# The second filter stage of batches 1 to 7: plain fp32 on four 64x64 squares of TensorE in place of 96x96 fp32r hi/lo products

## The chip, the cores and the metric

One core of a Trainium2 chip runs the whole program in one launch. The metric is device time in microseconds (us), from timed runs of one execution each; beside them stands one profiled execution, from which every duration here comes.

## The reference, cut to what matters

`x` is 8 batches of 3072 x 256 in fp32. Each of its columns is filtered along the sequence in the frequency domain, and two dense blocks of a feed-forward kind follow, token by token:

```
X = np.fft.rfft(x, axis=1)
Y = X * (filt_r + 1j * filt_i)[None, :, :]
y = np.fft.irfft(Y, n=3072, axis=1)
# block 1, on 24576 tokens
h = y @ w_in                        # 256 -> 1024
solu = h * softmax(h);  ln = (solu - mean) / sqrt(var + 1e-06) * g_ln
x2 = ln @ w_out                     # 1024 -> 256
# block 2
h = x2 @ w_in2                      # 256 -> 2048
out = (h / (1 + exp(-1.702 * h))) @ w_out2
```

## The kernel before, in words

**The transform.** 3072 is 128 x 24, and the real transform is done in two steps of small matrices. The first step multiplies 128 points by a 128 x 128 matrix (`step1`, line 493 in plain fp32, line 451 in three fp32r products); its result goes to a DRAM tensor `a_d`. That leaves 64 *slots* of 48 values (24 real, 24 imaginary) for the second step, whose matrices differ from slot to slot. Two slots make a *group* of R = 96 rows, 32 groups in all. Of a 96 x 96 matrix of a group half the entries are zero, since the two slots do not mix.

For each group of a pair of batches (1 and 2, 3 and 4, 5 and 6, then 7 alone) the second step does this: load the two matrices and the filter (`gt`) and the data (`bt`); split matrices and data in a high fp32r part and the rest (`split_m`, `split_a`: ScalarE copies, GpSimd subtracts); `forward`, one product of three fp32r matmuls at line 451 (high by high, rest by high, high by rest), into a PSUM tile of the tag `m`; two VectorE operations that weigh it with the filter (`xs`, `pr`); `swap`, two DMAs that exchange the halves of `xs`; `weigh`, an addition; `split_y`; `inverse`, again a product of three matmuls; a ScalarE copy `z` out of PSUM; `store_z`, a DMA to `z_d`. Both batches of a pair lie side by side, so a matmul has 512 columns (256 for batch 7). Batch 0 has its own class, `EarlyFilter`, in the opening.

**What follows.** A *piece* is 256 tokens; there are 96. `First` (one object for each piece) takes `z_d` through the last small transform (`y`, line 742) and block 1: `hidden` (line 760), softmax and norm on ScalarE and VectorE, a transpose by way of DRAM (`shuffle`, `gather`, `turn`), `project` (line 842), `x2_add`. `Second` does block 2 for two pieces at a time: `hidden` (line 913), `tanh`, `gate`, `split_hi`, `split_lo`, `output` (line 954).

**The order.** Nothing is scheduled at run time. Every step is put in a list with a planned time (`at`), the list is sorted once, and each engine gets its instructions in that order; an engine waits at its next instruction until the data is there. A unit of that time is a sixteenth of a piece. The tables FILTER and DENSE hold the planned times of the filter's steps: the second stage of batches 1 and 2 (DENSE) is spread over 8 pieces, four groups to a piece, and that of the later batches (FILTER) over 16 pieces, two groups to a piece. The tag `m` has two PSUM buffers, shared by the filter's products, by `y` and by `project`.

Nearly all loads and stores are issued by SyncE (SP), one after the other; a DMA whose data is not ready holds up those behind it.

Of the kernel before, what the change touches and what calls it, by code (L numbers as in the profile page):

```python
# [10 lines left out]
F32 = mybir.dt.float32  # L11
F32R = mybir.dt.float32r
# [14 lines left out]
NG = NSLOT // 2  # L27
FF1, FF2 = 1024, 2048
# [3 lines left out]
Q = 32  # L32
# [40 lines left out]
    "slots": (-0.4, 3.33, 4.15, 16.59),  # L73
    "first": (-9.95, -6.06, -1.85, 0.69),
    "second": (-7.28, -3.52, -2.25, 0.52, 1.17, 4.88, 12.1, 15.71, 20.24),
# [4 lines left out]
    "start": 15.68,  # L80
    "slots": (0.57, 4.18, 8.25, 12.02),
    "second": (-5.2, -2.91, -2.91, -0.1, 2.39, 5.33, 7.45, 10.13, 14.61),
# [51 lines left out]
def dft_constants():  # L134
# [15 lines left out]
    fwd1, inv1 = fwd1.reshape(N1, N1), inv1.reshape(N1, N1)  # L150
# [37 lines left out]
    fwd2 = fwd2.reshape(NG, R, R)  # L188
    inv2 = inv2.reshape(NG, R, R)
# [7 lines left out]
    def spread(m):  # L197
# [11 lines left out]
        [fwd1, inv1, turned, np.eye(N1), -np.eye(N1), blocks.reshape(P, -1)], 1)  # L209
    return [np.ascontiguousarray(a, np.float32) for a in (dft1, mats, sgn)]  # L210
# [3 lines left out]
def fft_filter_solu_gelu(  # L214
# [46 lines left out]
    mats_in = dft1[:, 4 * N1 + R:]  # L261
# [4 lines left out]
    sgn_sb = cst.tile([R, 2], F32, name="sgn_sb")  # L266
# [186 lines left out]
    filtered = [0] * B  # L453

    class Filter:
        pools = {"gt": [(p3, "gt")], "bt": [(p3, "bt")], "az": [(p2, "az")]}
        send = nc.sync.dma_start

        def __init__(self, batches):
# [10 lines left out]
            self.stored = 0  # L470
# [34 lines left out]
        def load2(self, g):  # L505
            self.load_gt(g)
            self.load_bt(g)

        def load_bt(self, g):
            assert self.stored == self.steps  # L510
            bt = self.tile("bt", g, [R, self.nb, D], F32)
            dma(out=bt, in_=self.a_d[:, g].rearrange("b r d -> r b d"))
            self.t[g]["bt"] = bt

        def load_gt(self, g):
            gt = self.tile("gt", g, [R, 2 * R + 2 * D], F32)
            dma(out=gt, in_=groups[:, g])
            fl = gt[:, 2 * R:].rearrange("p (t n) -> p t n", t=2)
            both = [R, self.nb, D]
            self.t[g] = dict(  # L520
                m=gt[:, :2 * R], fl=fl,
                fr=fl[:, 0:1].to_broadcast(both), fi=fl[:, 1:2].to_broadcast(both))

        def split_m(self, g):
            v = self.t[g]
# [3 lines left out]
            v["fwd"], v["inv"] = ([mt[:, i, j * R:(j + 1) * R] for i in range(2)] for j in range(2))  # L529

        def split_a(self, g):
            self.t[g]["a"] = split(self.t[g]["bt"], nc.gpsimd)

        def forward(self, g):
            v = self.t[g]
            f = ps_m.tile([R, self.nb, D], F32, tag="m", name="f2")
            product(f, v["fwd"], v["a"])
            xs = p2.tile([R, self.nb, D], F32, tag="xs", name="xs")
            pw = p2.tile([R, 2, self.nb, D], F32, tag="pw", name="pw")
            pr, v["xw"] = pw[:, 0], pw[:, 1]  # L540
            nc.vector.scalar_tensor_tensor(
                out=xs, in0=f, scalar=sgn_sb[:, min(g, 1):min(g, 1) + 1], in1=v["fi"],
                op0=ALU.mult, op1=ALU.mult)
            nc.vector.tensor_tensor(pr, f, v["fr"], op=ALU.mult)
            v.update(xs=xs, pr=pr)

        def swap(self, g):
            v = self.t[g]
            dma(out=v["xw"][:2 * N2], in_=v["xs"][2 * N2:])
            dma(out=v["xw"][2 * N2:], in_=v["xs"][:2 * N2])  # L550

        def weigh(self, g):
            v = self.t[g]
            nc.vector.tensor_tensor(v["pr"], v["xw"], v["pr"], op=ALU.add)

        def split_y(self, g):
            self.t[g]["y"] = split(self.t[g]["pr"], nc.vector)

        def inverse(self, g):
            v = self.t[g]  # L560
            f = ps_m.tile([R, self.nb, D], F32, tag="m", name="f3")
            product(f, v["inv"], v["y"])
            z = p2.tile([R, self.nb, D], F32, tag="az", name="z")
            nc.scalar.copy(out=z, in_=f)
            v["z"] = z

        def store_z(self, g):
            self.send(out=self.z_d[:, g].rearrange("b r d -> r b d"), in_=self.t.pop(g)["z"])
            for b in self.batches:
                filtered[b] += 1  # L570

    class EarlyFilter(Filter):
# [4 lines left out]
        def __init__(self, batches):  # L577
# [11 lines left out]
            bts = [pool.tile([P, 2 * D], F32, tag=tag, name="bt")  # L589
# [22 lines left out]
        def load_gt(self, g):  # L612
# [5 lines left out]
            if g % 2 == 0:  # L618
                dma(out=fl[:R // 2], in_=groups[:R // 2, g:g + 2, 2 * R:])
            if g == 0:  # L620
                dma(out=fl[H:W, 0], in_=groups[R // 2:, g, 2 * R:])
# [56 lines left out]
        def store_z(self, g):  # L678
# [4 lines left out]
            filtered[0] += 1  # L683

    def plan_filter(batches, first, second, early=None):


        f = Filter(batches) if batches[0] else EarlyFilter(batches)
        for i in range(f.steps):
# [415 lines left out]
```

## Time and profile before

| | |
|---|---|
| timed runs, three | 3632.44, 3633.64, 3636.73 us |
| median | 3633.64 us |
| the profiled execution: span from first to last instruction | 3631.5 us |
| its own time outside the span | not recorded; the median of the timed runs lies 2.1 us above the span |
| granted TensorE clock, mean | 0.994 |

The profile gives for each engine the time in which it had an instruction in work. A TensorE matmul's record begins when it is handed to the array and ends when its last column has left it, so records overlap: the distance from start to start is what a matmul costs, not the length of its record. An fp32r product is one matmul instruction, a plain fp32 product is two.

### The profile page before, as it was taken

What the parts mean: (1) busy time and instruction counts of PE and PEld (TensorE: products, weight loads), DVE (VectorE), ACT (ScalarE), POOL (GpSimd) and SP (SyncE); (2) the same over time, 40 slices, a digit from 0 to 9 for tenths busy, and PEclk for the clock granted to TensorE, in tenths of its full rate; (3) what the DMA queues carried; (4) which work ended last, traced back from release to release, by engine and by line L of the source; (5) the groups of instructions that cost most, each with busy time, mean ns of one, the idle gap of its engine ahead of it and who ended that gap; (6) DMA issues with size and microseconds to landing.
All of it is one profiled execution on the core that took longest, in us unless ns stands there. A gap on an engine that the chain in (4) does not pass through costs nothing.

```text
span 3631.5 us, 50437 instructions
## 1 busy us (share of the span) xinstructions
PE 3569.6 (98%) x16828; PEld 2942.3 (81%) x16828; DVE 2677.4 (74%) x3964; ACT 2034.3 (56%) x3672; POOL 795.5 (22%) x1315
## 2 busy tenths in 40 slices
PE   6899999999999999999999999999999999999999
PEld 4478888888888888888888888888888888888887
DVE  6878876677777777667777777667777776676665
ACT  3656655555555555555555555555555555555553
POOL 3033322212222221222222222211212111111110
PEclk8999999999999999999999999999999999999999
DMA  9855543434343433443434343333333332222221
GB/s 261 262 159 147 162 131 125 134 110 121 114 125 116 123 113 113 128 128 105 125 114 125 112 122 109 123 106 112 107 101 105 108 108 80 78 79 78 77 82 27
DMA packets 384597, 431.47 MB, mean 119 GB/s; under 512 B 143520, under 2 KB 294304, under 8 KB 384336
## 3 DMA queue, kind: packets, MB, share of 16 engines
q1 hardware_dynamic: 378704, 421.82, 39.3%
q10 hardware_dynamic: 5632, 6.42, 0.6%
q8 instruction: 132, 2.16, 0.3%
q14 instruction: 129, 1.06, 0.1%
HBM read 229.89 MB, written 176.16 MB: 112 GB/s over the span
## 4 chain that ended last, share of the span: by engine, by line
PE 92%; DVE 3%; DMA 2%; issue 1%; ACT 1%; SPq 0%; POOL 0%; DVEq 0%; ACTq 0%; POOLq 0%
PE o L954 28%; PE h L913 28%; PE x L842 15%; PE h L760 13%; PE f L451 5%; PE yt L742 2%; DMA a_d<-az 1%; PE f L671 0%; DMA e<-e_d 0%; DVE x2s L863 0%; PE f L493 0%; PE f L652 0%; DVE ob L965 0%; DVE e L785 0%; DVE gl L937 0%
## 5 line engine op out<-in xcount | busy, mean ns | idle before, releaser
L913 PE MATMUL h<-x2s,w 128*128 128x512 f32 (+1 forms) x4704 | 1179.4, 386 | 1.9 <-DVE th L925 1.3
L913 PEld LDWEIGHTS h<-x2s,w 128*128 128x128 f32 x4704 | 864.1, 188 | 180.6 <-DVE x2s L863 4.0
L954 PE MATMUL o<-gh,w 128*128 128x512 f32 (+1 forms) x3136 | 961.7, 388 | 4.2 <-DVE ob L965 3.3
L931 ACT CAST gh<-th 128x512 fp32r<-128x512 f32 x768 | 476.2, 620 | 684.2 <-DVE th L925 677.0
L954 PEld LDWEIGHTS o<-gh,w 128*128 128x128 f32 x3136 | 577.1, 188 | 121.2 <-issue 7.8
L954 PE MATMUL o<-gl,w 128*128 128x512 f32 (+1 forms) x1568 | 606.6, 387 | 2.0 <-DVE gl L937 2.0
L937 DVE TENSOR_TENSOR gl<-th,gh 128x512 fp32r<-128x512 f32 x768 | 559.3, 728 | 32.2 <-ACT gh L931 32.1
L925 DVE SCALAR_TENSOR_TENSOR th<-th,h 128x512 f32<-128x512 f32 x768 | 521.0, 678 | 29.1 <-ACT th L920 28.7
L920 ACT ACTIVATE th<-h 128x512 f32<-128x512 f32 x768 | 456.3, 594 | 107.4 <-PE h L913 106.7
L854 DVE TENSOR_TENSOR x_sum<-x,x_sum 128x256 f32<-128x256 f32 x192 | 81.5, 425 | 584.2 <-ACT x_sum L853 584.2
L842 PE MATMUL x<-u,w_hi 128*128 128x512 f32 x1536 | 383.1, 392 | 0.3 <-DVE u L833 0.3
L954 PEld LDWEIGHTS o<-gl,w 128*128 128x128 f32 x1568 | 294.8, 188 | 65.4 <-DVE gl L937 6.0
L842 PEld LDWEIGHTS x<-u,w_hi 128*128 128x128 f32 x1536 | 289.8, 189 | 62.6 <-DVE u L833 1.0
L776 POOL TENSOR_SCALAR q<-se 128x1 f32<-128x1 f32 x192 | 43.9, 229 | 1207.6 <-ACT e L772 1202.1
L805 DVE TENSOR_SCALAR e<-e,nmu,rs 128x1024 f32<-128x1024 f32 x192 | 160.7, 837 | 161.2 <-POOL rs L800 159.4
L853 ACT COPY x_sum<-x 128x256 f32<-128x256 f32 x192 | 71.0, 370 | 370.7 <-PE x L842 369.8
L796 ACT ACTIVATE h<-e,nmu 128x1024 f32<-128x1024 f32 x192 | 215.0, 1120 | 91.1 <-POOL nmu L788 91.0
L446 POOL TENSOR_TENSOR fl<-bt,fh 96x512 fp32r<-96x512 f32 (+1 forms) x128 | 175.2, 1368 | 365.1 <-ACT fh L445 346.5
L822 DVE STREAM_TRANSPOSE ut<-e 128x1024 f32<-128x1024 f32 x192 | 237.4, 1237 | 10.0 <-DMA e<-e_d 9.8
L766 DVE TENSOR_REDUCE nmx<-h 128x1 f32<-128x1024 f32 x192 | 234.3, 1221 | 13.6 <-PE h L760 13.5
L760 PE MATMUL h<-w_hi,xh 128*128 128x512 f32 x768 | 242.0, 396 | 0.0
L772 ACT ACTIVATE e<-h,nmx 128x1024 f32<-128x1024 f32 x192 | 214.2, 1116 | 44.6 <-DVE nmx L766 44.1
(99 smaller groups left out, 4691.1 us busy)
## 6 DMA issues: line engine op xcount, KB each, us to landing
e_d<-e SPq DMA_DIRECT2D x192, 512.0 KB, 3.0
e<-e_d SPq DMA_DIRECT2D x768, 128.0 KB, 3.0
gt<-in_groups SPq DMA_DIRECT2D x128, 264.0 KB, 3.7
zr<-z_d SPq DMA_DIRECT2D x96, 256.0 KB, 2.7
out<-ob SPq DMA_DIRECT2D x764, 32.0 KB, 1.6
bt<-a_d SPq DMA_DIRECT2D x112, 192.0 KB, 4.0
xin<-in_x SPq DMA_DIRECT2D x84, 256.0 KB, 3.4
a_d<-az SPq DMA_DIRECT2D x84, 256.0 KB, 2.7
```

Source lines behind the costliest of these rows:

```text
L760: nc.tensor.matmul(hs, xx[:, c, a * P:(a + 1) * P], ww[:, c, f * 512:(f + 1) * 512], start=(m == 0 and c == 0), stop=(m == 2 and c == 1))
L766: nc.vector.tensor_reduce(out=nmx, in_=self.h[a], op=ALU.max, axis=AX.X, negate=True)
L772: nc.scalar.activation(out=e, in_=self.h[a], func=AF.Exp, bias=self.v[a], accum_out=se)
L796: nc.scalar.activation(out=self.h.pop(a), in_=e, func=AF.Square, bias=nmu, accum_out=ssq)
L822: nc.vector.transpose(out=self.ut[a].rearrange("p k (i t) -> p k i t", t=Q), in_=self.e.pop(a).rearrange("p (i k f) -> p k i f", i=P // Q, ...
L842: nc.tensor.matmul(self.x2[c][:, :n].rearrange("p i t -> p (i t)"), w2[f][:, kk, c * P:(c + 1) * P], self.u[:, kk, :n].rearrange("p i a t ...
L913: nc.tensor.matmul(self.part(t, j), ww[:, c, f * P:(f + 1) * P], xx[..., c, :], start=(m == 0 and c == 0), stop=(m == 2 and c == 1))
L920: nc.scalar.activation(out=th, in_=self.t[d], func=AF.Tanh, scale=1.702)
L925: nc.vector.scalar_tensor_tensor(out=self.g[d], in0=self.g[d], scalar=1.0, in1=self.t.pop(d), op0=ALU.add, op1=ALU.mult)
L931: nc.scalar.copy(out=gh, in_=self.g[d])
L937: nc.vector.tensor_tensor(gl, th, gh, op=ALU.subtract)
L954: nc.tensor.matmul(o, ww[:, h, f], self.part(gg, j), start=(f == 0 and m == 0), stop=(f == K2 - 1 and m == 2))
```

## The change

For batches 1 to 7 the second stage goes by *quads* of four slots (two groups), q = 0 to 15:

- The four 48 x 48 matrices of a quad are stored so that each stands in its own 64 x 64 square of the array: slot w of group h uses rows from 64h and columns from 64w. `squares` issues four plain fp32 matmuls, one for each square, with 64 output columns, 48 rows (forward) or 64 (inverse) and 512 moving columns. The two that share their rows' half write to one PSUM tile, so a call takes both buffers of the tag `m`.
- Between forward and inverse, real and imaginary parts lie at distances of 32 partitions. `cross` (twice for a quad) is the pair of VectorE operations of before, on 128 partitions; `swap` is four DMAs of 32 partitions for each `cross`; `weigh` is unchanged in kind.
- `split_m`, `split_a` and `split_y` are gone.
- A quad is loaded by one DMA for the matrices, four for the filter (into one tile `fl_sb`, which is not doubled) and two for each batch for the data, and stored by four DMAs.
- The tables FILTER and DENSE give new planned times; DENSE has two quads to a piece, FILTER one. First-stage slots move a little.
- The tile that held the second output block of `finish` and some buffers of `EarlyFilter` change their tags.

```diff
 FILTER = {
-    "slots": (-0.4, 3.33, 4.15, 16.59),
-    "second": (-7.28, -3.52, -2.25, 0.52, 1.17, 4.88, 12.1, 15.71, 20.24),
+    "slots": (-0.05, 3.33, 4.15, 15.38),
+    "second": {"load2": -4.87, "forward": 3.89, "cross": (4.31, 5.2), "swap": (5.0, 5.69), "weigh": (8.13, 9.15), "inverse": 13.25, "copy_z": (14.01, 14.37), "store_z": 15.5},
 }
...
-        pools = {"gt": [(p3, "gt")], "bt": [(p3, "bt")], "az": [(p2, "az")]}
+        pools = {"gt": [(p4, "mt")], "bt": [(p2, "bt")], "az": [(p2, "az")]}
...
-        def split_m(self, g):
-            mt = p4.tile([R, 2, 2 * R], F32R, tag="mt", name="mt")
-            nc.scalar.copy(out=mt[:, 0], in_=v["m"])
-            nc.gpsimd.tensor_tensor(mt[:, 1], v["m"], mt[:, 0], op=ALU.subtract)
...
-        def split_a(self, g):
-            self.t[g]["a"] = split(self.t[g]["bt"], nc.gpsimd)
...
-            f = ps_m.tile([R, self.nb, D], F32, tag="m", name="f2")
-            product(f, v["fwd"], v["a"])
...
+        def load2(self, q):
+            gt = self.tile("gt", q, [P, 4 * H], F32)
+            dma(out=gt, in_=quads[:, q * 4 * H:(q + 1) * 4 * H])
+            fl = fl_sb
+            for w in range(2):
+                for b in range(2):
+                    to, of = w * H + b * Q, (2 * b + w) * N2
+                    dma(out=fl[to:to + N2], in_=groups[of:of + N2, 2 * q:2 * q + 2].rearrange(
+                        "i h (t d) -> i h t d", t=2))
+            bt = self.tile("bt", q, [P, 2, 2, D], F32)
+            for h in range(2):
+                for b in range(self.nb):
+                    dma(out=bt[h * H:h * H + 2 * N2, :, b],
+                        in_=self.a_d[b, 2 * q + h].rearrange("(w p) d -> p w d", w=2))
...
+        def squares(self, m, x, rows):
+            out = [ps_m.tile([P, self.nb, D], F32, tag="m", name="f2") for _ in range(2)]
+            for r in range(2):
+                part = slice(r * H, r * H + rows)
+                for c in range(2):
+                    nc.tensor.matmul(
+                        out[r][c * H:(c + 1) * H], m[part, c * H:(c + 1) * H], x(r, c)[part],
+                        start=True, stop=True, skip_group_check=True)
+            return out
+
+        def forward(self, q):
+            v["f"] = self.squares(v["fwd"], lambda h, w: v["bt"][:, w, :self.nb], 2 * N2)
...
+        def swap(self, q, h):
+            for k in range(P // Q):
+                to, of = k * Q, (k ^ 1) * Q
+                dma(out=v["xw", h][to:to + Q], in_=v["xs", h][of:of + Q])
...
+        def inverse(self, q):
+            v["f"] = self.squares(v["inv"], lambda w, h: v["pr", h], H)
+
+        def copy_z(self, q, w):
+            v["z", w] = p2.tile([P, self.nb, D], F32, tag="az", name="z")
+            nc.scalar.copy(out=v["z", w], in_=v["f"][w])
```

TensorE in the dense stage before, about one piece into it. `f` on line 451 are the filter's products, `h` and `o` block 2, `yt` the last small transform. Each product stands by itself among the others' matmuls:

```order
465 L451 MATMUL f_2806<-fh,mt 96x512 x2
466 L451 MATMUL f_2806<-fl,mt 96x512
467 L913 MATMUL h_2812<-x2s,w_740 128x512 x6
468 L954 MATMUL o<-gh,w_788 128x512 x2
469 L954 MATMUL o<-gl,w_788 128x512
470 L954 MATMUL o<-gh,w_788 128x512 x2
471 L954 MATMUL o<-gl,w_788 128x512
472 L913 MATMUL h_2856<-x2s,w_740 128x512 x6
473 L451 MATMUL f_2864<-fh,mt 96x512 x2
474 L451 MATMUL f_2864<-fl,mt 96x512
475 L742 MATMUL yt<-first,zr 128x128 x4
```

The same engine and stage now. Line 549 is `squares`: `f<-pw` an inverse, `f<-bt` a forward, a row for each of the call's two PSUM tiles; line 888 is `project`, line 806 block 1's `hidden`. Two stretches of one piece:

```order
399 L549 MATMUL f_2421<-pw,gt 64x512 x2
400 L549 MATMUL f_2422<-pw,gt 64x512 x2
401 L549 MATMUL f_2433<-bt,gt 64x512 x2
402 L549 MATMUL f_2434<-bt,gt 64x512 x2
403 L806 MATMUL h<-w_hi,xh 128x512 x2
...
421 L549 MATMUL f_2564<-pw,gt 64x512 x2
422 L549 MATMUL f_2565<-pw,gt 64x512 x2
423 L888 MATMUL x_2570<-u,w_hi 128x512 x8
```

An inverse, which holds both buffers of the tag `m`, now stands directly before a forward in one place of the piece and directly before `project` in the other, and both of these write to the tag `m`.

SyncE's queue in the dense stage before, half a piece. `pw<-xs` is `swap`, `gt` and `bt` the loads, `z_d` the store, `e_d<-e` and `e<-e_d` are `shuffle` and `gather` of block 1:

```order
229 L549 DMA pw<-xs 48x512
230 L550 DMA pw<-xs 48x512
231 L517 DMA gt<-in_groups 96x704
232 L512 DMA bt<-a_d_138 96x2x256
233 L568 DMA z_d_139<-z 96x2x256 x2
```

The same queue now:

```order
182 L577 DMA pw<-xs 32x512 x8
183 L525 DMA gt<-in_dft 128x256
184 L530 DMA fl_sb<-in_groups 24x1024 x4
185 L535 DMA bt<-a_d_138 48x2x256 x4
186 L858 DMA e_d<-e 128x1024
187 L864 DMA e<-e_d 32x4x256 x4
188 L577 DMA pw<-xs 32x512 x8
189 L596 DMA z_d_139<-z 48x2x256 x4
```

From one `zr` load to the next but one, two pieces of the dense stage, the queue held 78 DMAs and now holds 122; in a stretch with one quad to a piece it held 58 and now holds 80.

## Rows read from the trace of the kernel before

**Rows 1.** The page's part 1: busy time, share, instructions.
```profile
PE 3569.6 (98%) x16828; PEld 2942.3 (81%) x16828; DVE 2677.4 (74%) x3964; ACT 2034.3 (56%) x3672; POOL 795.5 (22%) x1315
```

**Rows 2.** Busy time by stretches: length, then busy time of each engine, clock.
```profile
0.00:120.00 120.00, 82.87 (x274) 51.70 (x275) 80.56 (x141) 57.51 (x117) 32.91 (x44) 0.89 0.93 264
...
360.00:480.00 120.00, 120.00 (x562) 98.00 (x561) 103.10 (x151) 74.64 (x141) 45.14 (x55) 1.00 0.54 154
```

**Rows 3.** The chain that ended last: share of the span by line.
```profile
by line: PE o L954 27.6%; PE h L913 27.6%; PE x L842 14.7%; PE h L760 13.1%; PE f L451 5.4%; PE yt L742 2.2%; issue 1.0%; DMA a_d<-az 0.5%; PE f L671 0.4%; DMA e<-e_d 0.4%; DVE x2s L863 0.4%; PE f L493 0.4%; PE f L652 0.4%; DVE ob L965 0.4%
```

**Rows 4.** Groups of instructions by shape, line 451: count after the shape.
```profile
L451 PE MATMUL f<-fh,mt 96*96 96x512 f32 x384 | 121.7, 398 | 0.8 <-POOL mt L528 0.6 <-DVE x_sum L854 0.2
L451 PE MATMUL f<-fh,fwd 128*128 128x512 f32 x120 | 37.8, 396 | 0.0
L451 PE MATMUL f<-fh,mt 96*96 96x256 f32 x128 | 25.0, 282 | 0.0
```

**Rows 5.** TensorE in order of time, two products of 512 columns: start, length.
```profile
1722.45 0.63 PE L451 MATMUL f<-fh,mt 96*96 96x512 f32 x2
...
1723.15 0.62 PE L451 MATMUL f<-fh,mt 96*96 96x512 f32 x2
...
1723.84 0.62 PE L760 MATMUL h<-w_hi,xh 128*128 128x512 f32 x2
```

**Rows 6.** The same, two products of 256 columns.
```profile
2625.89 0.40 PE L451 MATMUL f<-fh,mt 96*96 96x256 f32 x2
...
2626.59 0.63 PE L760 MATMUL h<-w_hi,xh 128*128 128x512 f32 x2
```

**Rows 7.** The same, a plain fp32 product of 512 columns, then fp32r.
```profile
139.53 0.59 PE L493 MATMUL f<-xin,first 128*128 128x512 f32 x1
139.97 0.59 PE L493 MATMUL f<-xin,first 128*128 128x512 f32 x1
140.00 0.80 PE L760 MATMUL h<-w_hi,xh 128*128 128x512 f32 x1
140.63 0.40 PE L760 MATMUL h<-w_hi,xh 128*128 128x512 f32 x1
```

**Rows 8.** The same, an fp32 product that begins after a wait.
```profile
144.58 1.12 PE L412 MATMUL w_lo<-w_top,unit 128*128 128x512 f32 x2 [1.31 <-ACT w L415]
```

**Rows 9.** The same, four fp32 products of 128 columns, and what follows.
```profile
1716.06 1.05 PE L742 MATMUL yt<-first,zr 128*128 128x128 f32 x8
1716.87 0.70 PE L954 MATMUL o<-gh,w 128*128 128x512 f32 x2
```

**Rows 10.** The same at the start of the dense stage: waits in brackets.
```profile
249.29 0.47 PE L451 MATMUL f<-fh,mt 96*96 96x512 f32 x1 [0.63 <-POOL mt L528]
250.52 0.47 PE L451 MATMUL f<-fl,mt 96*96 96x512 f32 x1 [0.76 <-POOL fl L446]
```

**Rows 11.** Groups by shape: busy time, mean ns of one, idle before.
```profile
L564 ACT COPY z<-f 96x512 f32<-96x512 f32 x96 | 55.8, 581 | 44.9 <-PE f L451 42.0
L446 POOL TENSOR_TENSOR fl<-bt,fh 96x512 fp32r<-96x512 f32 x96 | 151.6, 1579 | 240.0 <-ACT fh L445 221.4 <-PE o L954 18.6
```

**Rows 12.** SyncE in the dense stage, in order of time: start, length.
```profile
371.17 0.51 SPq L549 DMA_DIRECT2D pw<-xs  x1
371.73 0.59 SPq L550 DMA_DIRECT2D pw<-xs  x1
```

**Rows 13.** Waits of SyncE's queue from 260 to 560: us in total, times, longest.
```profile
SPq L736 <- DVE x2s L863: 63.8, 8, 9.4
SPq L812 <- DVE e L805: 34.5, 13, 5.5
...
SPq L818 <- DMA e_d<-e: 19.2, 10, 3.6
```

**Rows 14.** The chain that ended last, in order of time: `project` in two successive pieces.
```profile
340.86 2.79 PE x L842 x16
380.32 2.77 PE x L842 x16
```

More of the change, by code (lines that the diff above doesn't have):

```diff
@@ L27 @@
 NG = NSLOT // 2
+NQ = NG // 2
 FF1, FF2 = 1024, 2048
@@ L503, in store_a @@
             self.stored += 1
[L505 to L522, printed above, removed]
@@ L559, in inverse @@
[L559 to L568, printed above, removed]
+            nc.vector.tensor_tensor(pw[:, 0], f, v["fr"][h], op=ALU.mult)
@@ L683, in store_z, with plan_transform @@
             filtered[0] += 1
-    def plan_filter(batches, first, second, early=None):
-        f = Filter(batches) if batches[0] else EarlyFilter(batches)
+    def plan_transform(f, first):
         for i in range(f.steps):
@@ L692, in plan_filter, with plan_early @@
                 at(t, step, i)
+    def plan_early(batches, first, second, early):
+        f = EarlyFilter(batches)
+        plan_transform(f, first)
         for g in range(NG):
             steps = (
-                f.load_bt if early else f.load2, f.split_m, f.split_a, f.forward, f.swap, f.weigh,
+                f.load_bt, f.split_m, f.split_a, f.forward, f.swap, f.weigh,
                 f.split_y, f.inverse, f.store_z)
@@ L701, in plan_filter @@
                 at(t, step, g)
-            if early:
-                in_order(early(g), second(g)[1])
-                at(early(g), f.load_gt, g)
+            in_order(early(g), second(g)[1])
+            at(early(g), f.load_gt, g)
+    def plan_filter(batches, first, second):
+        f = Filter(batches)
+        plan_transform(f, first)
+        for q in range(NQ):
+            v = second(q)
+            in_order(v["load2"], v["forward"])
+            for k in range(2):
+                in_order(
+                    v["forward"], *(v[name][k] for name in ("cross", "swap", "weigh")),
+                    v["inverse"], v["copy_z"][k], v["store_z"])
+            for name in ("load2", "forward", "inverse", "store_z"):
+                at(v[name], getattr(f, name), q)
+            for name in ("cross", "swap", "weigh", "copy_z"):
+                for k in range(2):
+                    at(v[name][k], getattr(f, name), q, k)
     def segments(start, count):
@@ L1018, in fft_filter_solu_gelu, with later, second @@
     at(v["small"][1], lambda: dma(out=sgn_sb, in_=sgn))
-    def dense(g):
-        p, k = divmod(g, len(DENSE["slots"]))
-        return [16.0 * p + DENSE["start"] + DENSE["slots"][k] + d for d in DENSE["second"]]
+    def later(start, steps):
+        def second(q):
+            move = lambda t: [move(x) for x in t] if isinstance(t, tuple) else start + 16.0 * q + t
+            return {name: move(t) for name, t in steps.items()}
+        return second
     def ahead(i):
@@ L1028, in ahead, with dense @@
         return [t + dt for dt in v["more"]]
+    def dense(q):
+        n, k = divmod(q, len(DENSE["second"]))
+        return later(DENSE["start"] + 16.0 * (n - q), DENSE["second"][k])(q)
     plan_filter(together[1], ahead, dense)
@@ L1034, in piece @@
             return 16.0 * ((batches[0] - 2) * NPAIR - 1 + i // 4) + FILTER["slots"][i % 4]
[L1036 to L1041 removed]
+        start = 16.0 * ((batches[0] - 2) * NPAIR - 1 + len(batches) * N2 // 8)
+        plan_filter(
+            batches, lambda i: [piece(i - 4) + d for d in FILTER["first"]],
+            later(start, FILTER["second"]))
     at(v["unit"], load_unit)
```

110 lines of the change are left out of this document (68 added, 42 removed).

## The prediction

> **What bounds the kernel now.** I read the page's first part, then the stretches, then the chain. TensorE has something in work for 98% of the span; the other engines are far from it, VectorE 74%, ScalarE 56%, GpSimd 22% [rows 1]. Records of matmuls overlap, so a full TensorE could hide short waits; the stretches say where there are any. In the first 120 us it is busy for 82.87, at a granted clock of 0.89; from 360 on it is busy for 120.00 of 120.00 at 1.00 [rows 2]. The reader is to see in the chain that its entries are nearly all TensorE lines, and that line 451, the first and second filter stage together, holds 5.4% of 3631.5 us, 196 us [rows 3]. So the change is worth what it does to TensorE's own time, and what it adds in waits of TensorE.
>
> **What it removes.** A product of three fp32r matmuls costs 0.695 us at 512 columns: two of them go from 1722.45 to 1723.84 [rows 5]. At 256 columns two go from 2625.89 to 2626.59, 0.35 each [rows 6]. The second stage has 384 / 2 = 192 products of the first size and 128 / 2 = 64 of the second; 60 more of the first size belong to the first stage and stay [rows 4]. Removed: 192 x 0.695 + 64 x 0.35 = 155.8 us. The chain's 196 less 60 x 0.695 leaves 154.5; the two agree. The splits that go too (GpSimd 1.58 us each [rows 11], ScalarE, VectorE) stand beside a full TensorE and are worth nothing there, but for one place: at the dense stage's start TensorE waits 0.63 and 0.76 us for GpSimd's splits [rows 10], and these 1.4 us go.
>
> **What it adds on TensorE.** Three batch pairs of 16 quads, twice each, are 96 calls of `squares` with 512 columns; batch 7 has 32 with 256. A call is four plain fp32 products, two matmul instructions each. One such product alone costs 0.87 us: its halves begin at 139.53 and 139.97, and behind the second the next matmul's columns end where its successor begins, at 140.63, so they took their 0.23 from 140.40 on [rows 7]. Fewer columns cost in proportion: eight halves of 128 columns take 0.81 us, 0.10 each [rows 9]; 0.44 for 256.
>
> No row shows two matmuls on different squares at once. The ends are one product's time a call, 0.87 us, if the four run side by side, and four, 3.48 us, if they don't. What bears on it is how a matmul is handed over. In [rows 7] the fp32r matmul at 140.00 was handed to the array 0.03 us after the one before it had begun, 0.40 us before it could stream (its record is 0.80 long, its successor's 0.40). So a matmul can wait at the array and needn't hold the queue. If each square has such a place, the second half of one square's product waits there, the next square's first half goes past it, and the call takes 0.87. I take that as likeliest, and 0.87: 96 x 0.87 + 32 x 0.44 = 97.6 us.
>
> The Trainium skill, TensorEngine Tiling (Array Packing), Key Properties, says that tiles operate independently and can load weights and multiply in parallel; by that rule a call is one product's 0.87 us. No run here shows it. The same section says that a change of the tiling mode drains TensorE; that has no row either.
>
> A call changes from the full array to squares and back, 256 changes in all. The nearest row is a stream that begins again after a wait: its fp32 product's records reach 1.12 us [rows 8], against 139.97 + 0.59 - 139.53 = 1.03 in a full stream [rows 7]; 0.10 us, weights that nothing covers. Below, a change costs nothing. Above, the last matmul also runs out before the next begins: a record of 0.39 less the 0.23 to its successor [rows 5], 0.16, so 0.26 a change. I take 0.10, the row's own: 256 x 0.10 = 25.6 us (0 to 66.6).
>
> **What it adds in waits.** A call holds both buffers of the tag `m`. In the sparse pieces several matmuls of block 2 lie between any two users of the tag, and I count nothing; without that cover a copy's 0.58 us would be paid 48 times, 28 us. In the dense stage the order shows an inverse directly before a forward (7 times) and directly before `project` (8 times). There TensorE waits for ScalarE's copy `z`, 0.58 us [rows 11], once before `project` and twice before a forward, whose second tile needs the second copy: 8 x 0.58 + 7 x 1.16 = 12.8 us. Everything in TensorE's queue stands behind that, block 2 too. Nothing of it, if the copies find cover, is the lower end. VectorE does six operations a quad as before, on 128 partitions in place of 96, and loses two; `fl_sb` is filled anew only after the second `cross`, which SyncE waits for; in DENSE the refill is planned at least five units ahead of its forward, so I count nothing.
>
> **The sum.** -155.8 - 1.4 + 97.6 + 25.6 + 12.8 = -21.2 us on a span of 3631.5: 3610.3. The timed median lies 2.1 us above the span, which I carry over: 3612 us. With the lower ends of both unknown prices it is 3574; with the upper price of a change, 3653. A change must cost under 0.18 us for the kernel to gain.
>
> **Rivals.**
> *Matmuls enter in strict order (slower).* Place: inside `squares`. The two halves of a product use one square, and in [rows 7] the second begins 0.44 after the first; it is not handed over early. If it holds the queue meanwhile, the next square's first half begins only with it. Then a second half and the next first half run together, and a call takes five halves, 5 x 0.435 = 2.18 us. 96 x 2.18 + 32 x 1.09 + 25.6 = 269.8; the dense copies hide behind the second pair of squares: +112.6, 3746 us. For it: the 0.44. Against: the early handing over at 140.00. It decides from 1.17 us a call on, where the gain is gone. The Trainium skill, TensorE: Matmul & The Clock Gate, What overlaps and what doesn't, says that matmuls start and end strictly in program order and only weight loads are pulled ahead; by that rule this rival comes out. The trace agrees as far as every later matmul in it begins later, which a full array would show in either case.
> *The upper and lower half of the rows have queues of their own, the two squares of a half do not.* A call takes three halves, 1.31 us: 96 x 1.31 + 32 x 0.65 + 25.6 + 12.8 - 157.2 = +27.8, 3661 us. No row is for or against it.
> *The squares don't run together at all,* so that the change doesn't do what it says: 96 x 3.48 + 32 x 1.74 + 25.6 - 157.2 = +258, 3892 us. For it: the trace has no overlap of this kind. Against: each of the four has a quarter of the array, and a PSUM region, to itself.
> *SyncE's queue bounds the dense stage.* DMAs start 0.56 us apart when nothing holds them [rows 12]. A dense piece has 61 in place of 39, 34.2 us of some 39.5 (380.32 - 340.86 [rows 14]). Its waits for the norm and for `shuffle`'s landing, 34.5 and 19.2 us over 300 us [rows 13], are 7 us a piece: 41 in all, against 39.9 that TensorE then needs (39.5 - 8 x 0.695 + 4 x 1.07 + 1.74). If each of the four `swap`s also waits for its pair on VectorE, about 1.4 us, it is 47. Eight pieces late by 1 to 7 us are 10 to 55; at the middle 3645 us. For it: the sum is so near. Against: the longest wait there now, 63.8 us for the last reader of `zr`'s tile, is slack, and the sparse pieces have 40 DMAs, only 22 us.
>
> **How the numbers follow.** The forecast has a chance of 0.55, strict order 0.25, queues by halves 0.08, no overlap 0.04, SyncE 0.08. 0.2% is 7 us, about what a measurement of this kernel can tell from no change. Within the forecast, gains over 7 us need a change of mode under 0.16 us or cover for the copies: 0.44 of the 0.55, with 0.06 within 7 us and 0.05 slower. SyncE's case gives 0.02, 0.03 and 0.03; the other three are slower. Faster 0.46, same 0.09, slower 0.45. The forecast's own range is 3585 to 3645; with strict order let in, 3585 to 3752, which leaves out the squares one by one, the cheapest changes of mode and the upper edge of strict order.
>
> **What would show it.** The start-to-start times in a call: eight halves in 0.87 us, four records starting within a few hundredths, is the forecast; starts at 0, 0.44, 0.44, 0.87, 0.87 and so on is strict order; eight starts 0.44 apart is no overlap. The distance from the last block matmul to the first square and back gives the price of a change. Idle time of `project` and of forwards between 250 and 560 us, ended by the copies `z`, should come to some 13 us and nowhere else. On SyncE, a late `gather` in that stretch would show as VectorE's transposes waiting for it. The prediction is wrong if a call takes over 1.17 us, or if TensorE's idle time in the sparse stretches is no longer near zero.

## The result, and the profile after

The changed kernel takes 3658.41 us (median of four runs, 3657.52 to 3660.02) against 3634.48 for the kernel before: a ratio of 1.0066, 95% interval 1.0052 to 1.0080. It is slower by 24 us; the prediction was 3612 us, faster. The span of the profiled execution went from 3631.5 to 3655.7 us, by 24.2, and that is what is explained here.

The page's part 1 of the changed kernel (busy time, share, instructions), to be held against [rows 1]:

```profile
PE 3573.1 (98%) x17084; PEld 2847.4 (78%) x17084; DVE 2562.9 (70%) x3836; ACT 1884.5 (52%) x3288; POOL 496.0 (14%) x1060
```

All other engines have less to do than before, and TensorE's record time hardly moved. The loss is not in these sums. The same two stretches as in [rows 2] say where to look (length, busy time of each engine, granted clock, DMA share, GB/s):

```profile
0.00:120.00 120.00, 84.52 (x279) 52.67 (x280) 81.79 (x143) 58.18 (x118) 34.98 (x45) 0.89 0.92 267
360.00:480.00 120.00, 113.30 (x528) 79.66 (x528) 83.54 (x125) 52.70 (x92) 10.33 (x26) 0.99 0.53 146
```

TensorE was busy for 120.00 us of the second stretch before and is busy for 113.30 now. That is the dense stage, in which batches 1 and 2 get their second filter stage. In the chain by line, the second stage has a line of its own now (549) and the first stage is at 466; both were line 451 in [rows 3]:

```profile
by line: PE o L1000 26.9%; PE h L959 26.6%; PE x L888 14.5%; PE h L806 13.3%; PE f L549 3.3%; PE yt L788 1.9%; issue 1.6%; PE f L466 1.1%; DMA a_d<-az 0.5%; DVE ob L1011 0.5%; DVE e L831 0.5%; SPq L577 0.4%; DMA e<-e_d 0.4%; DMA bt<-a_d 0.4
```

The groups that answer to [rows 4] and to the copy in [rows 11] (count, busy time, mean ns, idle time before them and what ended it):

```profile
L549 PE MATMUL f<-pw,gt 64*64 64x512 f32 x384 | 59.4, 639 | 2.1 <-DVE pw L581 0.8 <-ACT z L590 0.7
L549 PE MATMUL f<-bt,gt 48*64 48x512 f32 x384 | 55.9, 614 | 4.8 <-ACT z L590 4.0 <-DMA bt<-a_d 0.8
...
L590 ACT COPY z<-f 128x512 f32<-128x512 f32 x96 | 52.3, 588 | 21.1 <-PE f L549 21.1
```

**One call of `squares` in a sparse stage**, TensorE in order of time (start, length), the answer to [rows 5]:

```profile
1017.93 0.39 PE L1000 MATMUL o<-gl,w 128*128 128x512 f32 x1
1018.25 1.09 PE L549 MATMUL f<-pw,gt 64*64 64x512 f32 x8
1019.27 1.65 PE L959 MATMUL h<-x2s,w 128*128 128x512 f32 x6
1020.75 0.62 PE L1000 MATMUL o<-gh,w 128*128 128x512 f32 x2
```

From 1017.93 to 1020.75 are 2.82 us. In a full stream the first row costs 0.23 and the six of line 959 cost 1.36 (401.68 to 403.07 and 404.43 to 405.79 in the same trace are 1.39 and 1.36), so 1.23 us are left for the call. The same call in two narrow windows, and TensorE's weight loads around it (PEld):

```profile
1018.25 0.66 PE L549 MATMUL f<-pw,gt 64*64 64x512 f32 x4
```
```profile
1018.73 0.61 PE L549 MATMUL f<-pw,gt 64*64 64x512 f32 x4
```
```profile
1017.71 0.19 PEld L1000 LDWEIGHTS o<-gl,w 128*128 128x128 f32 x1
1018.25 0.21 PEld L549 LDWEIGHTS f<-pw,gt 64*64 64x64 f32 x8 [0.35 <-issue]
1019.26 0.53 PEld L959 LDWEIGHTS h<-x2s,w 128*128 128x128 f32 x3 [0.81 <-issue]
```

Four halves begin together, the other four together 0.48 us later. The squares do run side by side, as forecast. The 0.36 us above 0.87 lie mostly at the call's two ends: 0.09 before it (0.32 from the matmul ahead in place of 0.23), 0.04 between its halves (0.48 in place of 0.44), 0.22 behind it (0.54 from its last halves to line 959 in place of 0.44, and 1.48 for the six there in place of 1.36). The weight loads show the same: in the stream the weights of the matmul at 1017.93 load from 1017.71, 0.22 us ahead of it, while those of the squares and those of the block behind them load only when their own matmul is handed over. A call of batch 7, the answer to [rows 6]:

```profile
2602.89 0.39 PE L1000 MATMUL o<-gl,w 128*128 128x512 f32 x1
2603.21 0.66 PE L549 MATMUL f<-pw,gt 64*64 64x256 f32 x8
2603.80 1.65 PE L959 MATMUL h<-x2s,w 128*128 128x512 f32 x6
2605.29 0.62 PE L1000 MATMUL o<-gh,w 128*128 128x512 f32 x2
```

Here 2.40 - 1.59 = 0.81 us are left.

**Loss by stage.** `project` runs once for each piece, so the start of its first matmul in piece n, after against before, tells how late the kernel is by then. This table is worked out from the starts of the 96 pieces (pieces counted from 0):

```
                               before       after    late by   gained or lost
piece 2  (dense stage begins)   224.73      223.24     -1.5     -1.5
piece 10 (dense stage over)     535.82      570.92    +35.1    +36.6
piece 58 (batches 3 to 6 over) 2280.30     2304.60    +24.3    -10.8
piece 62 (batch 7 begins)      2423.97     2448.25    +24.3      0.0
piece 78 (batch 7 over)        2990.41     3013.69    +23.3     -1.0
```

So the change gains 11.8 us where it was to gain, and loses 36.6 in eight dense pieces. A dense piece of before is 39.45 us long [rows 14]; now pieces of 45.6 and 42.8 us alternate. The long one, from `project` to `project` (the bracket is idle time of TensorE and what ended it):

```profile
398.77 2.12 PE L888 MATMUL x<-u,w_hi 128*128 128x512 f32 x8 [0.66 <-ACT z L590]
...
412.75 1.09 PE L549 MATMUL f<-bt,gt 48*64 48x512 f32 x8
...
417.13 1.65 PE L959 MATMUL h<-x2s,w 128*128 128x512 f32 x6 [0.33 <-DVE th L971]
...
423.81 0.73 PE L806 MATMUL h<-w_hi,xl 128*128 128x512 f32 x2 [0.27 <-DVE xl L797]
425.85 0.81 PE L1000 MATMUL o<-gh,w 128*128 128x512 f32 x2 [1.31 <-DVE ob L1011]
...
428.33 1.74 PE L549 MATMUL f<-pw,gt 64*64 64x512 f32 x8
430.75 1.56 PE L549 MATMUL f<-bt,gt 48*64 48x512 f32 x8 [0.68 <-ACT z L590]
432.25 0.73 PE L806 MATMUL h<-w_hi,xh 128*128 128x512 f32 x2
...
442.17 1.59 PE L549 MATMUL f<-pw,gt 64*64 64x512 f32 x8
444.43 0.96 PE L888 MATMUL x<-u,w_hi 128*128 128x512 f32 x3 [0.66 <-ACT z L590]
```

Two kinds of wait stand here. Behind both inverse calls (428.33, 442.17) the next user of the tag `m` waits for ScalarE's copy, as predicted. The wait before the forward is longer than its bracket. Two narrow windows of the call at 430.75:

```profile
430.75 0.65 PE L549 MATMUL f<-bt,gt 48*64 48x512 f32 x2 [0.68 <-ACT z L590]
```
```profile
431.24 1.08 PE L549 MATMUL f<-bt,gt 48*64 48x512 f32 x6
```

Only the two products of the first tile begin at 430.75; those of the second tile begin 0.49 us later, when the second copy is done (all four begin together in the call at 1018.25). That part is no idle time, since the first tile's products run meanwhile. But behind the forward call at 412.75 three matmuls wait for VectorE, which none did before. VectorE in that place, in order of time:

```profile
413.88 0.75 DVE L566 SCALAR_TENSOR_TENSOR xs<-f,sgn_sb,fl_sb 128x512 f32<-128x512 f32 x1 [0.55 <-PE f L549]
414.55 0.68 DVE L569 TENSOR_TENSOR pw<-f,fl_sb 128x512 f32<-128x512 f32 x1
415.14 0.74 DVE L566 SCALAR_TENSOR_TENSOR xs<-f,sgn_sb,fl_sb 128x512 f32<-128x512 f32 x1
415.80 0.68 DVE L569 TENSOR_TENSOR pw<-f,fl_sb 128x512 f32<-128x512 f32 x1
416.40 0.68 DVE L971 SCALAR_TENSOR_TENSOR th<-th,h 128x512 f32<-128x512 f32 x1
```

It waits 0.55 us for the call to end and then does the four operations of the two `cross` steps in one row, 2.5 us. Block 2's `th` (416.40) stands behind them, and the matmul at 417.13 behind that; `xl` comes late behind the same row. The wait for the output block `ob`, 1.31 us, is another matter: it stays in full when the row is halved (11 below) and is 0.3 us when the inverse calls are placed apart (3). After that idle time the granted clock is lower (two stretches of 2 us; the column behind the five engines):

```profile
424.00:426.00 2.00, 0.69 (x3) 0.28 (x3) 2.00 (x6) 0.00 (x0) 0.00 (x0) 1.00 0.84 260
426.00:428.00 2.00, 2.00 (x6) 1.27 (x6) 2.00 (x4) 1.04 (x2) 0.00 (x0) 0.57 0.45 178
```

The waits of TensorE from 260 to 570 us (sum, times, longest), all of which are 0 or nearly so before:

```profile
PE x L888 <- ACT z L590: 4.6, 7, 0.7
PE f L549 <- ACT z L590: 4.0, 6, 0.7
PE o L1000 <- DVE ob L1011: 3.9, 3, 1.3
PE h L959 <- DVE th L971: 2.3, 7, 0.3
PE h L806 <- DVE xl L797: 1.9, 7, 0.3
```

They are 16.7 us in sum; a wait also slows the matmuls behind it (the six at 417.13 have a record of 1.65 us, the six at 401.68 one of 1.55), so it costs more than its idle time. SyncE's waits in the same stretch, against [rows 13]: 41.5 us for `x2s` (63.8 before), 23.1 for `shuffle`'s landing (19.2) and 3.2 for the norm (34.5). VectorE's transposes, in which the prediction wanted to see a late `gather`, wait 0.7 us for it.

### The profile page after: what moved, and what is told of

Its sections match the earlier page's. It is cut to its first block, busy times and chain, and to the rows that moved or that the text cites. A ratio compares the mean times of both kernels' runs of the same rounds, so it can differ in the third digit from the quotient of the medians.

```text
span 3655.7 us, 50697 instructions
## 1 busy us (share of the span) xinstructions
PE 3573.1 (98%) x17084; PEld 2847.4 (78%) x17084; DVE 2562.9 (70%) x3836; ACT 1884.5 (52%) x3288; POOL 496.0 (14%) x1060
## 4 chain that ended last, share of the span: by engine, by line
PE 89%; DVE 4%; DMA 3%; issue 2%; SPq 1%; ACT 1%; POOL 1%; DVEq 0%; ACTq 0%; POOLq 0%
PE o L1000 27%; PE h L959 27%; PE x L888 15%; PE h L806 13%; PE f L549 3%; PE yt L788 2%; PE f L466 1%; DMA a_d<-az 1%; DVE ob L1011 0%; DVE e L831 0%; SPq L577 0%; DMA e<-e_d 0%; DMA bt<-a_d 0%; ACT h L842 0%; DMA pw<-xs 0%
## 5 line engine op out<-in xcount | busy, mean ns | idle before, releaser
L983 DVE TENSOR_TENSOR gl<-th,gh 128x512 fp32r<-128x512 f32 x768 | 529.1, 689 | 32.3 <-ACT gh L977 32.2
L812 DVE TENSOR_REDUCE nmx<-h 128x1 f32<-128x1024 f32 x192 | 234.5, 1222 | 15.4 <-PE h L806 15.0
L806 PE MATMUL h<-w_hi,xl 128*128 128x512 f32 x768 | 238.0, 391 | 1.9 <-DVE xl L797 1.9
```

The lines of the kernel that those rows point to most:

```text
L806: nc.tensor.matmul(hs, xx[:, c, a * P:(a + 1) * P], ww[:, c, f * 512:(f + 1) * 512], start=(m == 0 and c == 0), stop=(m == 2 and c == 1))
L812: nc.vector.tensor_reduce(out=nmx, in_=self.h[a], op=ALU.max, axis=AX.X, negate=True)
L983: nc.vector.tensor_tensor(gl, th, gh, op=ALU.subtract)
```

## The experiments

Theories. **A**: the loss comes from the dense stage alone, where (A1) both buffers of `m` are held by a call and come free late, and (A2) the four VectorE operations stand in a row ahead of block 1 and block 2. **B**: the squares cost that much wherever they stand. **C**: SyncE's queue, fuller by 22 DMAs a piece. **D**: the latency from forward by way of `swap` to `weigh`. Some expectations use these letters. Times, ratios to the kernel before with their intervals, and the loss between piece 2 and piece 10, read as above from the trace of each:

```
                                         us   ratio [95% interval]       dense loss
the changed kernel                   3658.4   1.0066 [1.0052, 1.0080]        36.6
1 old product in batches 1, 2        3705.6   1.0188 [1.0173, 1.0204]         0.6
2 the same, buffers kept apart       3619.4   0.9957 [0.9942, 0.9972]         0.6
3 inverse calls placed apart         3644.4   1.0028 [1.0018, 1.0037]        23.1
4 VectorE's pairs placed apart       3713.6   1.0212 [1.0196, 1.0227]        91.2
5 both                               3700.4   1.0175 [1.0158, 1.0192]        74.8
6 all calls placed anew              3656.6   1.0064 [1.0047, 1.0081]        33.8
7 swaps issued by GpSimd             3659.1   1.0065 [1.0048, 1.0082]        35.0
8 the same, on 3                     3657.1   1.0062 [1.0047, 1.0077]        32.5
9 loads issued by GpSimd             3678.7   1.0119 [1.0104, 1.0134]        46.3
10 no swaps                          3653.8   1.0052 [1.0037, 1.0067]        31.6
11 no swaps, no swapped part         3639.5   1.0015 [1.0005, 1.0024]        17.0
12 the same, on 3                    3631.5   0.9990 [0.9981, 0.9999]         7.8
13 on 2: full array, batches 3 to 6  3597.6   0.9898 [0.9881, 0.9914]        -0.5
```

**Is it the dense stage alone? (1, 2)** Batches 1 and 2 get back the old groups, product and planned times; the others keep the squares.

```diff
-    plan_filter(together[1], ahead, dense)
+    plan_groups(together[1], ahead, dense_groups)
```

> Batches 1 and 2 go through the second stage of the kernel before (96x96 fp32r groups, its planned times); batches 3 to 7 through the squares. Theory A, the whole loss arises in the dense stage and the squares gain elsewhere: the sparse stretches keep their 11.8 us of gain (35.2 less 29.7, 29.8 less 24.3, 24.3 less 23.3 in the table of pieces), so about 3623 us. Theory B, the squares cost time wherever they stand: no better than the kernel before, 3634 us or more.

The dense pieces were 39.45 us again, but each sparse piece lost. The output block `ob` had gone back to the buffers of the tag `xs`, which `cross` uses too, and from 600 us on TensorE waited 52.1 us in 40 places for `gl` behind it on VectorE. That was my edit and not the question, so it was run again with a buffer of its own for `ob`:

> As e4_hybrid, but the second output block of finish keeps its own buffer, as in the changed kernel (e4_hybrid had put it back on a tag that the squares' cross uses, and lost 1.5 to 4 us in each sparse piece for it). Theory A, the loss is the dense stage's alone: dense pieces at 39.45 us, sparse pieces at 36.21, some 4 us for the 32 more DMAs and the opening: 3623 to 3628 us. Theory B, squares cost time wherever they stand: 3634 us or more.

3619.4 us: faster than both kernels, by 0.43% against the kernel before. TensorE in the dense stage is full again (stretch of 90 us in this kernel):

```profile
330.00:420.00 90.00, 90.00 (x419) 73.33 (x418) 78.34 (x114) 55.19 (x104) 33.08 (x40) 1.00 0.54 154
```

So B falls: the pieces with squares are as long as in the changed kernel (36.21 us, 36.56 before), and the loss belongs to the dense stage. Between pieces 10 and 58 this kernel gains 13.2 us and the changed kernel 10.8; the other 2.4 come from pieces in which no call of `squares` stands (36.44 us against 36.65), for a reason that was not looked into.

**Buffers and VectorE by placement (3 to 6).** The planned times alone were changed. In 3 the inverse calls stand so that a block lies between each and the next user of `m`; in 4 the second `cross`, `swap` and `weigh` of a quad stand later; 5 does both; 6 moves forwards as well.

```diff
-"inverse": 9.05, "copy_z": (9.9, 10.2), "store_z": 10.64}, ... "inverse": 18.9,
+"inverse": 10.78, "copy_z": (11.28, 11.58), "store_z": 12.38}, ... "inverse": 18.02,
```

> Only the dense stage's inverses, their copies and stores are planned elsewhere, so that a block of other matmuls stands between an inverse and the next user of the tag m. Theory A1, the waits for the copies and for the sums in front of the inverse (1.43 and 0.99 us a piece, eight pieces) are one part and VectorE's lateness another: 19 us less, 3639 us. Theory A2, VectorE is late because TensorE was held up: both go, 3617 to 3625 us. Theory C, SyncE's queue of 61 DMAs a piece bounds the dense stage: no change, 3658 us.

The dense loss fell by 13.5 us. The wait of `project` for the copy is gone, that of the forwards is down to 1.8 us; `th` and `xl` are waited for as before (2.3 and 2.0 us). The wait for `ob` fell from 3.9 to 0.9 us. A1 is a cause, and not the only one.

> Only the two VectorE pairs (cross) of a quad in the dense stage are planned apart, with a gate and a split_lo of block 2 between them, and with them swap, the second weigh and the loads; inverses stay beside the next user of m. Theory A1: VectorE's part of the loss goes, some 24 us, 3635 us. Theory A2: no more than a few us, since TensorE is still held up by the copies. Theory C: no change, 3658 us.

> Both moves together, and the first quad's forward half a piece block later. Theories A1 and A2: a dense piece falls below the 39.45 us of before, by 4 x 0.16 us a piece as in the sparse stretches, so 3617 us in all. Theory C: no change, 3658 us.

Both were far off. With the second pair late, its `weigh` is late and the inverse call waits for it (4, waits of TensorE from 260 to 570 us):

```profile
PE f L549 <- DVE pw L581: 28.4, 14, 5.9
```

The row of four is not free to be pulled apart: a quad's inverse needs both pairs, and each has `swap`'s DMAs behind it. So I also moved the calls themselves:

> The changed kernel with the whole dense plan of the four-slot stage moved: each forward and inverse call stands so that a block lies before the next user of its output buffers, and the four operations of a forward call are spread over VectorE's idle stretches instead of lying four in a row ahead of the next block's norms. Theory A (the dense loss of 36.6 us is output buffers that come free late plus VectorE's four operations ahead of the norms): dense loss falls to at most 15 us, so 3617 to 3637 us, and the rows that wait for th, xl and ob in 260 to 570 us go below 3 us together (8 us in the changed kernel). Rival (the squares themselves cost in this stage, or the granted clock falls for another reason): 3640 us or more, and pieces of 41 us and over against 39.45.

A miss as well. `th`, `xl` and `ob` are no longer waited for, but other waits are in their place (TensorE's, then one of VectorE):

```profile
PE x L888 <- DVE pw L569: 7.7, 6, 1.3
PE f L549 <- DVE pw L581: 5.5, 6, 2.1
```
```profile
DVE pw L581 <- DMA pw<-xs: 56.3, 16, 6.4
```

`project` now waits for `cross` to read the forward's tiles, and `weigh` waits for the swap with all of VectorE's queue behind it. Two buffers of `m` and one queue of VectorE: the wait moves, it does not go.

**SyncE's queue (7 to 9).** Theory C, the rival of the prediction too.

```diff
-                dma(out=v["xw", h][to:to + Q], in_=v["xs", h][of:of + Q])
+                (nc.gpsimd.dma_start if self.batches[0] == 1 else dma)(
+                    out=v["xw", h][to:to + Q], in_=v["xs", h][of:of + Q])
```

> The changed kernel, with the 16 swap DMAs of a dense piece issued by GpSimd in place of SyncE; planned times untouched. Theory C, the time from forward to inverse is SyncE's (eight DMAs at 0.63 us behind each cross, loads behind them): VectorE and TensorE wait less, most of the 36.5 us of the dense stage goes, 3625 to 3635 us. Theory A, copies and VectorE's own work are the cause: within 5 us of 3658 us.

> e1_apart (inverses planned apart from the next users of the tag m) with the dense swaps issued by GpSimd too. Theory C with A: both causes of the dense waits are gone, dense pieces near 38.9 us, 3617 to 3622 us. Theory A alone: as e1_apart, 3644 us.

> The changed kernel, with the 18 load DMAs of a dense piece (matrices, filter, data) issued by GpSimd in place of SyncE. Theory C, if it is the count of DMAs in SyncE's queue: 18 of 61 leave it, as good as moving the swaps, 3625 to 3635 us. Theory C2, if it is the time of one quad's eight swaps and not the queue's length: little, 3650 us or more. Theory A: within 5 us of 3658 us.

With 16 DMAs a piece fewer on SyncE the time is the same, and TensorE's five waits are those of the changed kernel to 0.1 us. On the kernel with the inverse calls apart (8) it made things worse: there TensorE waits 8.8 us for `gl`, 1.8 in 3, while the wait for the norm is as in 3; why was not settled. With the loads in place of the swaps (9) it was worse still: GpSimd's part of the norm then stands behind the DMAs that it issues (ScalarE waits 27.1 us for `nmu` in 9, 7.0 in the changed kernel). So C is not what costs the 36.6 us; 10, in which these 16 DMAs are on no queue at all, is 5.0 us better.

**VectorE's row and the swap by leaving them out (10 to 12).** In 10 `weigh` adds without a swap; in 11 the operation that makes `xs` goes too; 12 is 11 with the placement of 3.

```diff
+            if self.batches[0] != 1:
+                nc.vector.scalar_tensor_tensor(
+                    out=xs, in0=f, scalar=sgn_sb[:, col:col + 1], in1=v["fi"][h],
+                    op0=ALU.mult, op1=ALU.mult)
...
+            if self.batches[0] == 1:
+                v["xw", h] = v["pr", h]
+                return
```

> The changed kernel with the eight swap transfers of each dense call left out (the filter's weigh adds the unswapped product, so that part of the filter is not computed for batches 1 and 2). Theory A: the transfers only matter where an inverse call waits for weigh, about 0.4 us a call, so 3652 to 3658 us, dense pieces still 45 and 42.5 us. Rival D (the latency of forward, cross, swap, weigh is what stretches the dense stage): 3620 to 3635 us, dense pieces near 40 us.

> As the kernel without the dense swaps, and also without the operation that makes the swapped part (two VectorE operations of 0.75 us less in each dense call, so 1.5 us of the 2.84 us row; that part of the filter is not computed for batches 1 and 2). Theory A: VectorE's row ahead of the next block's norms is half as long, so 8 to 15 us less than the kernel without swaps: 3638 to 3650 us, and the granted clock stays at 0.9 or more where it fell to 0.57. If VectorE's row were without effect: the same time as the kernel without swaps within 3 us.

Without swaps the dense loss falls by 5.0 us, so D is a small part at most. Without the two operations it falls by 14.6 more. All that TensorE still waits for in that stage (11):

```profile
PE x L894 <- ACT z L596: 4.6, 7, 0.7
PE f L549 <- ACT z L596: 4.0, 6, 0.7
PE o L1006 <- DVE ob L1017: 4.0, 3, 1.3
```

`th` and `xl` are gone from the list, and the copies and `ob` stand as they were. A2 is shown, at up to 14.6 us, for the granted clock differs too: it is 1.00 in each 90 us from 240 on, against 0.98 in the changed kernel.

**The granted clock in these comparisons.** Between piece 2 and piece 10 TensorE stands at the lower of its two levels (1.2 GHz) for 18.7 us in the changed kernel, 11.7 in 3, 7.5 in 10, none in 11, and 4.0 in the kernel before. At the higher level (2.4 GHz) the same columns would take about half of that (the first and second halves of the call at 428.33 begin 0.91 us apart, those of the call at 1018.25 0.48), which gives an estimate of the most that it costs. So the clock can be up to 3.8 of the 14.6 us, up to 3.5 of the 13.5 of kernel 3, and all of the 5.0 that leaving out the swaps gave back. The clock's fall doesn't follow from the wait for `ob` alone. That wait of 1.31 us stands three times in the changed kernel, in 7, in 10 and in 11, and the clock falls behind three, two, one and none of them. One such wait in 11, and the stretch from 415 to 417 us there:

```profile
413.48 0.70 PE L1006 MATMUL o<-gh,w 128*128 128x512 f32 x2 [1.32 <-DVE ob L1017]
```
```profile
415.00:417.00 2.00, 1.33 (x11) 0.36 (x12) 1.83 (x3) 1.49 (x4) 0.00 (x0) 1.00 0.88 235
```

Both relieved at once (12):

> The dense stage with both relieved: no swapped part and no swap (as the kernel without them; that part of the filter is not computed for batches 1 and 2), and each inverse call placed so that a block stands between it and the next user of its output buffers. Theory A says that the two causes are apart and add up: the kernel without the swapped part measured 3639.5 us, the placement alone was worth 14 us, so 3622 to 3630 us, within 5 us of the kernel in which batches 1 and 2 keep the old product (3619.4), and dense pieces of 39 to 41 us. Rival: one cause seen twice, so 3636 to 3642 us.

7.8 us of loss are left. The placement took 9.2 us here and 13.5 alone; the row and the swap 15.3 here and 19.6 alone. Together 28.8, where a plain sum would be 33.1: two causes that mostly add up, with 4.3 us that either takes away. The measured 3631.5 lies 1.5 above the range that I gave for that.

**The change of mode (13).** On kernel 2, a call of batches 3 to 6 is replaced by two plain fp32 products over the whole array with half the columns.

```diff
+            if self.nb == 2:
+                for r in range(2):
+                    nc.tensor.matmul(out[r][:, 0], m, x(r, 0)[:, 0], start=True, stop=True)
+                return [o[:, 0:1].to_broadcast([P, 2, D]) for o in out]
```

> On the kernel in which batches 1 and 2 keep the old product (3619.4 us): in batches 3 to 6 each call of four squares gives way to two plain fp32 products over the whole array with half the columns each, so the same columns in stream (2 x 0.44 us) and no change of mode before or after (the filter of these batches is not computed; the forward call multiplies the matrices by themselves). If the 0.36 us that a call takes above its 0.87 us is the change of mode, 64 calls give back 23 us: 3594 to 3600 us. With the price that the prediction took (0.10 a change) 12.8 us: 3604 to 3609 us. If the 0.36 us comes from the plain fp32 product itself (its weights, its two halves), nothing: 3617 to 3622 us.

21.8 us less than kernel 2, 0.34 us for each of 64 calls, or 0.17 a change (by the profiled spans, 3619.0 and 3600.1, it is 0.30 and 0.15; between pieces 10 and 58 it is 19.6 us, 0.31 and 0.15). TensorE in order of time, one such call:

```profile
1016.15 0.40 PE L1097 MATMUL o<-gl,w 128*128 128x512 f32 x1
1016.39 1.02 PE L556 MATMUL f<-pw,gt 128*128 128x256 f32 x4
1017.06 1.75 PE L1056 MATMUL h<-x2s,w 128*128 128x512 f32 x6
1018.65 0.62 PE L1097 MATMUL o<-gh,w 128*128 128x512 f32 x2
```

2.50 - 1.59 = 0.91 us, against 1.23 for the squares; the first half begins 0.24 behind the matmul before it, as in a full stream, where the squares' begins 0.32 behind. These calls also have four matmul instructions in place of eight, which the experiment doesn't separate from the change of mode; the rows at 1018.25, with 0.31 of the 0.36 us at the call's ends, speak for the change.

## Why the prediction was wrong, point by point

- *TensorE bounds the kernel, and what is removed is worth 155.8 us.* Right. In the sparse stages 64 calls gained 10.8 us, so a call costs 1.39 - 0.17 = 1.22 us there if two products were worth 2 x 0.695; the row of the call says 1.23.
- *Four squares run side by side, 0.87 us.* Right. The rivals of strict order, of queues by halves and of no overlap fall with the two rows at 1018.25 and 1018.73; the same columns over the full array take 0.91. Queues by halves gave 3661 us, the nearest of all to the measured 3658, and that is chance.
- *A change of mode costs 0.10 us.* Mis-sized. The row gives 0.18 and the experiment 0.15 to 0.17, inside the bounds of 0 to 0.26, but about at the price that the prediction named as the one up to which the kernel gains. For 192 changes at 0.18 that is 15 us more. Batch 7 doesn't fit: its call reads 0.81 us, 0.11 more than the 0.70 removed, and yet the stage gained 1.0 us. Part of it is block 2, which before was held up a little by `x2s` in that stage and no longer is: its 768 matmuls `h` there cost 0.232 us each before, 0.228 in batches 3 to 6, together 3 us. The rest stays open.
- *The copies in the dense stage cost 12.8 us.* Right in place and size: they are 8.6 us of idle time, and in the six forward calls behind them the second tile waits 0.48 us more, 11.5 in all. Moving the inverse calls gave back 13.5, with the wait for `ob` and part of the clock in it.
- *VectorE does six operations a quad as before; I count nothing.* This step failed, and with it the count of waits, 28.9 us too few. It counted VectorE's work (which did fall, from 74% to 70%) and not where it stands. Before, a group's two operations waited for one product and stood among others; now four stand in one row behind one call, ahead of `th` and of block 1's norm, in a stage whose slack was too small for 2.5 us. Leaving out half of the row and the swap behind it gave back 19.6 us. The prediction also had no term for the granted clock: 18.7 us at the lower level against 4.0 before, up to 7 us of the 36.6.
- *SyncE bounds the dense stage (rival).* Wrong mechanism: it gave 3645, and the queue could be relieved of 16 DMAs a piece without effect.
- The sum. The dense stage should have gained 32 x (1.39 - 1.23) = 5 us by its calls and lost 36.6, so its waits are 41.7 where 12.8 were counted, 28.9 too few. With 15.4 for the changes of mode and 0.9 for batch 7 that makes 45.2 of the 45.4 us between -21.2 and +24.2. Of the 41.7, the experiments take away 28.8, the clock's part included; the other 12.9 are left in kernel 12. Its trace shows where: between piece 2 and piece 10 TensorE is idle for 8.4 us, 3.1 before, and 6.9 us lie inside calls whose second tile waits behind the first. In the changed kernel the same two counts are 24.6 and 11.0, part of them at the lower clock. The row below is such a call of kernel 12, to be held against the 1.09 of a free one.
- The range. 3585 to 3752 us holds the measured time, but only because it was widened for strict order, which didn't come; the forecast's own range ended at 3645.

```profile
411.84 2.05 PE L549 MATMUL f<-bt,gt 48*64 48x512 f32 x8 [0.58 <-ACT z L596]
```

Each error alone would have left the kernel close to where it was: with the measured price of a change and 12.8 us of waits the sum is -6 us, with the measured waits and the predicted price +8.

## What to carry to other kernels

Count the changes of TensorE's mode and price them from a call in the trace: here two of them cost 0.31 to 0.36 us around 0.87 us of columns, and the call saves 0.16 us of the 0.52 that its columns alone would. When steps are merged into larger calls, look at what each in-order engine does in the microseconds after the call, since a row of operations that is no longer spread delays whatever stands behind it, however idle that engine is on average. A change can pay in one stage and not in another: the version with the old product in the full stage and the squares in the sparse ones, 3619.4 us, beats both kernels.

## What the hardware showed that was not expected

- The order of matmuls is not strict between squares. Each of the four products is two instructions on one square, and four of the eight begin together at 1018.25, the other four at 1018.73: each square has begun its first half before any begins its second. The Trainium skill, TensorE: Matmul & The Clock Gate, What overlaps and what doesn't, has matmuls start and end strictly in program order; these two rows differ from it where the matmuls use different squares, if the two halves of a product stand next to each other in the program. Nor is another order strict: in the held call at 430.75 the second halves of the first tile begin at 431.24, 0.48 us behind their first halves as in the free call, though the first halves of the second tile begin only then.
- The Trainium skill, TensorEngine Tiling (Array Packing), Key Properties, says that a change of mode drains TensorE and gives no price. The runs agree with a drain: the weights of the new mode load only when the matmuls of the old one are nearly out (1018.25 and 1019.26 above), and a change costs 0.15 to 0.18 us at 512 columns.
- A single idle time of 1.31 us was followed by 4 us of a granted clock of 0.57 (426 to 430 us), near the lower of the two levels, 1.2 and 2.4 GHz; the same idle time in kernel 11 was followed by a clock of 1.00.
